# Query halves, transposed probabilities and attention's output of the first sub-blocks: copied by ScalarE instead of VectorE, under new order strings

## The chip, the cores and the metric

One core of one Trainium2 chip runs the program. The time is that of one execution on the device, in microseconds (us). Engines: PE (TensorE: matmuls; PEld are its weight loads), DVE (VectorE), ACT (ScalarE), POOL (GpSimd) and SP, whose queue issues most DMAs.

## What is computed

Chunked attention with 8 memory keys feeds a gated mixing layer and a feed-forward layer with a residual. Batch 4, sequence 768, model width 512, 8 heads of 64.

```python
for c in range(nc):                                   # chunks of 32 queries
    q_c = q[:, :, c_start:c_end]
    k_full = np.concatenate([mem_k, k_ctx], axis=2)   # 8 + 16 + 32 + 8 keys
    v_full = np.concatenate([mem_v, v_ctx], axis=2)
    scores = scale * np.matmul(q_c, k_full.transpose(0, 1, 3, 2))
    scores = scores - np.max(scores, axis=-1, keepdims=True)
    a = np.exp(scores)
    a = a / (np.sum(a, axis=-1, keepdims=True) + 1e-09)
    out[:, :, c_start:c_end] = np.matmul(a, v_full)
...
gate = 1.0 / (1.0 + np.exp(-gate_pre))                # gate_pre: 5 taps over time
x = gate * (x @ w_val) @ w_out
...
xn = (x - mu) / np.sqrt(var + 1e-06) * g_ln
ch = np.maximum(xn @ w_ch1, 0.0) @ w_ch2
return (x + ch).astype(np.float32)
```

## The kernel before

The sequence is cut into 24 sub-blocks of 128 tokens (n = 0 to 23). They form blocks: block 0 is sub-block 0, block 1 is sub-blocks 1 and 2, block 2 is 3 and 4, block 3 is 5 and 6, and so on. Each block goes through attention, mixing (`mix_steps`) and the feed-forward layer (`ch1` fills c_ps, `second` fills acc).

Matmuls of later blocks take float16 halves: each value is a high and a low half, and three products stand for one. The weights arrive as 64-bit numbers in 20 pieces of 1 MB. Each piece is made a 32-bit one (`to_f32`: ScalarE L239, then VectorE L240), goes into a sum of squares (`gram`: matmuls that add into a Gram matrix, whose trace `weight_scale` takes on VectorE as diag, L293, and a column, L294, and sums on PE, L301), and is split into halves (`split_weight`: ScalarE L310, VectorE L311). While that goes on, the first blocks work on 32-bit data: attention of sub-blocks 0 to 4 (`attention32`), mixing of blocks 0 and 1, the feed-forward layer of block 0 (its input is xnf).

`attention32` copies the queries into a block-diagonal tile bd (two halves of 64 partitions: the first by ScalarE at L482, the second by VectorE at L484 unless `n in BD`), takes scores (s_ps) on PE, exponentials (sc), transposes the probabilities on PE (pT_ps, L498), copies them to pT (VectorE L505, or ScalarE if `n in PT`), and multiplies them with the values (pv, L515). `activations` writes pv out to xT in four pieces of 64 partitions: two by ScalarE (L413); the other two by ScalarE if `n < EVAC_ACT or n >= NEVAC`, else by VectorE (L415). `split_values` uses the same function for sub-blocks 5 and later, with a scale.

At the start, and behind the first scores, the program has fills: 120 matmuls on a tile of ones (L269) whose result nobody reads (32 + 64 + 8 + 16, `FILLS`).

What sets the order: the program is recorded in the order of `PLAN`, and then `pin` chains the instructions of each engine in an order that is written out as a string per engine (`ORDER`). A letter in it is the stream that an instruction belongs to (a and b: attention of even and odd sub-blocks, x and y: mixing, f and g: feed-forward, m, p, q: weights, s: set-up), a number how many follow, and `+n` takes one from further back in its stream. Each engine executes its string strictly in order.

Of the kernel before, what the change touches and what calls it, by code (L numbers as in the profile page):

```python
# [54 lines left out]
ORDER = {
    "PE": (
        "s24a+16a+16a+16a+16a+16a+16a+16a+16a+16a+16a+16a69a+4a+4a+4a+4a+4a+4a+4a+4a+20a+20a+20a+20a+20a+20a+20a+20a+20a+20a+20"
        "a+20a+20a+20a+20a+20a20m16m+16x14b16x2m8x4m8a16b14s8p8b6p16a4mx4p16a16f3f+13f+13f+13f13p8y3f6p8y13p8y2pb17y6f20gf15g5q16"
        "b4gaf4a16qg4b16ff+23g3f23a4g2a16bf23g12f27x12b48f21g6f24g6x7f36x29g11f12gx6ax18f12g6b48f12g24a48g30f48a48bg18f72b48y36"
        "g24ay12g6f24b48y24a48g6f36g12f12g6a48g24bx12f48x12f48x24b48f48g30af36b48g12f12a48x24g60bg12a48g54f96g10b48g20y24f48y24a"  # L60
        "f24g12b48f24a48y24g30bg66a48g30b48x24f60x12f12x12f24g18f48g12ag24b48f12g18a48x24f36g30bg42a48g24f24b48f60y12g10f12y36g32"
        "f36ag12f24b48f24a48y24g6f12g42bg36a48g30b48f96x36f12x12f12g10f12g8f12g12ag24b48f36a48x24f12g60bg54a48f72b48f24y48f12g10"
        "f24g20f12b48ag24f24a48y18f12y6f12g18ba48g96f96b48g10x24g8x24f48g12ag24b48f24g6a48x24f24g78ba48g30f96g10b48y48g32f24g18"
        "f24b48g24y24f12g12f36x48g72f96g42f48g18x12f12g42f36g36f36g6f48g12f12g12f60g48f36g48"),
    "DVE": (
        "sa4s3a5m2bm+2m+2mxx+3xx+2xx+1x3x+3xx+2x4mx2mb2pb2abm+2mbmxpxaxbaxpxax2axax5maxp2axmp2a2b+3yy+3yy+2myy+1y2pyy+3yqyy+1yqym"
        "yqy2mp3mp4bq2b+2b2ypbmy2mybyqybymya+3ybypy2qybypyqypybqpq2x+20qyqaa+2a2q2paq2ayaqapaqb2pqax+22gqb3fbqb3a2b2afqtxtxty+20x"
        "bx2bfb+6btxfx+2xx+1tt+2xtfxbxtxtxbtxtxtbtfxbtx2qxa2t+1t3btxtax2txt+2xax2tx3fax3ax2ab2xaxa+8xatafxa3ta2t2atbt2y+22gt+1tgf"
        "b3fb3a2bt2ytby2fy2tytytx+20y2y+3aybtbyy+1y2tt+1bytbtfbyfbta2tyabya2bya2b2taa+7t+1tyfay2x+22at2yay2ay2ayayty3tay3tt+2tyf2"
        "ybt3yaxgtbtb2txtxt+1x2gy+20xbxtb3fxfxfx+3f2bxfx+2xb+7x2b2f3bf2b2xbfxx+1ba2xafafa3fafa+7xfa2ba4fxax5y+22x10f3xf3b2xy2b2"  # L70
        "y+2yy+1bg4g+1g2babf3x+20f2bfb+8b2fy2fyfyb4yf2y2by2fby2a3fayfy+1a3f2ay2fa+8x+22a2fa4yaby3aby3b2fy5fy4f3yb3fb2yag2b+7b2gxg"
        "g+1g2xx+2xx+1b3xfxfxf3bxx+3fx2x+1x3f6bxy+20a3x+1xaxa4f2a+7fa2bfay+22afa2x7fx6ax4b4f5xfb4g4g+1g2yayb+7y+2f2yy+1fyf2byby2"
        "y+3yfyy+1y3f3bfbyfb2fby+1a2ya6f2yfa+7f2a2fa4by5x+20x+22y9ay2f2b2yfb4f2byfbgxg3g+1g2b+8baxx+2f2bf3xx+1fx3b2x2f2xbfxfbx2f"
        "x2bfbxx+1a5f2af2ax2faa+8a2fa5xbx2y+20xax12f3xy+22f2b2fbxb4g4g+1g2y2y+2aybfb+7fbfby+1y2fyfyx+20b2fy+3b2y2y+1f5y2byfyy+1y2"
        "a3f2a5f2a+7fa2ba4fx+22ay8by2by6f2bfbfybfx2x+2yfxx+1bx2g4g+1g2bxbf5afb+7b2fbxbf2bx+3xbfxx+1xfxbxy+20fxx+1a4f2a2fxf2a2a+7a"
        "xa3fa2x11ax2y+22x4bf5b4xbfg4g+1gx+20gy2bf2bay+2byf3b+8b2fy+1y4y+3byfyb4fy+1yfy2byfy+1f2y2x2yf3yf2xx+1y3x2y5by6fyf5yfx+2x"
        "x+1xg4g+1g2f6xfx+1xfx2f3x5f2x14f3xf10g4g+1gf2g5"),
    "Activation": (
        "s3asam3a4x2bx2mpxbaxp3ab3p3bb+1a2y3pqymm+1q2fbyqq+2qmpya+1q+1qbypqmfaq+1qpq+1qfpypqb+3pfyqpaq2b+3b2pqfqb2qa2b2fbxaqfb+2x"
        "abfxt+1a2ftxfqx3t+1bta2xfxt+1b2atfa+2x2ab2at+1btbf2ab2a2ybb+2fy3t+1tf2aba2y2ba3yb2fa+2t+1ty2ab3fat+1yfta4yax2b2t+1btbx2"  # L80
        "f+1f2b+2f3afba2fxbf+1fx2fa3a+2b6afxaxb2f+1f2x3fxa4y2b2gybab+2f+1f6ba2yafbf+1f2ya3y2b4a+2b2fbaybyf+1af2b2y2bfya2ya3gb+2x3"
        "bf+1f2xf4bxa2faf+1fxfxa3a+2b6axbxfbaf+1x2f2bxbxfa4bgyb+2a2y2f+1fyf2bf3a2yfbyf+1ya3f2a+2b4fbabyf+1yb2fafy2b2y2fba5gxb+2x"
        "a3f+1f3xbfxf3bxf+1f2a2x2aa+2b3fb2af+1xbaxfbfbx3fxb3ga4y3af+1yf2b+2a3bf4bfyf+1y2f2b2a3a+2b4fabay2bf+1f2aby2a3x2y2fb2gb+2a"
        "f+1f6ax2b2afaxf+1f2xa3b4a+2xfax2bf+1afx2fb3x2fa3b2ga2y2bb+2f+1f3bf2y2fbyfb2y2b2f+1x2f2by2xfy2f+1fxfy2fgf+1f7x3f+1f2x3f"
        "f+1f5gf2"),
    "Pool": (
        "s2as2s+2s2ab2a+1ab4atga+1ba2b3a+1a2bab2"),
    "SP": (
        "s+1s3w2l2w2l2w2lw4l3wqw2lqwql2wlqay2ay2a+1a2gb+2ab+2b+2b2x2a+2x2a+2a+2a2b+2b+2gb3ga+2a+2a+2a2y4b+2b+2g2b+2b2a+2a+2a+2a2"
        "x4b+2b+2gb+2b2a+2a+2ga+2a2y4b+2b+2gb+2b2ga+2a+2a+2a2x4b+2b+2b+2bg2ba+2a+2a+2a2y4b+2b+2b+2b2g2a+2a+2a+2a2x4b+2b+2b+2b2a+2"  # L90
        "g2a+2a+2a2y4b+2g2b+2b+2b2a2x4b2g2y4g2x2g4"),
}
# [1034 lines left out]
```

## Time and profile before

| | |
|---|---|
| median of 3 runs | 715.03 us (713.51 to 715.72) |
| the profiled execution's own time | 715.32 us |
| its span, first to last instruction | 713.2 us |
| PE busy | 699.4 us, 98% |
| VectorE busy | 617.2 us, 87% |
| ScalarE busy | 466.4 us, 65% |

The busy share is an average over stages. A matmul of 32-bit data stands in the trace as two records. The span's first 100 us hold the loading and the conversion of the weights; what is read from the trace there is in the rows below, of which each group says what its columns are.

### The profile page before, as it was taken

Reading aid. Unit: us, or ns where it says so; the run is one execution under the profiler, and the core shown is the slowest. Engines: PE = TensorE matmul, PEld = TensorE weight load, DVE = VectorE, ACT = ScalarE, POOL = GpSimd, SP = SyncE. Lnnn points to the kernel's source line nnn. Section 1 sums busy time; section 2 is a strip of 40 time slices with the busy share of each in tenths; the row PEclk is TensorE's granted clock in tenths of the full one; section 3 lists DMA queues with packets and bytes.
Section 4 is the critical chain, followed back from the end, with each engine's and each line's share of the span. In section 5 each row is a group of like instructions: output and inputs, shape, how many; then the busy total and the mean of one; then the engine's idle time right before and its main releaser. Section 6 shows DMA issues by size and latency. Waiting matters only on the chain.

```text
span 713.2 us, 18043 instructions
## 1 busy us (share of the span) xinstructions
PE 699.4 (98%) x7581; PEld 566.8 (79%) x7581; DVE 617.2 (87%) x1341; ACT 466.4 (65%) x746; POOL 16.5 (2%) x37
## 2 busy tenths in 40 slices
PE   8799999999999999999999999999999999999998
PEld 7697668657568788888888878878888878878897
DVE  4999999999999989989889998989988978866643
ACT  3679986556666885873875786677784765553330
POOL 2010010000000000000000000000000000000000
PEclk9999999999999999999999999999999999999999
DMA  9998232041423322323322332232233120111001
GB/s 346 417 409 336 60 96 98 16 112 53 113 59 97 82 46 83 81 55 90 91 52 68 86 73 68 74 83 68 65 87 90 31 31 17 46 17 45 1 17 46
DMA packets 64449, 67.76 MB, mean 95 GB/s; under 512 B 47856, under 2 KB 48112, under 8 KB 64368
## 3 DMA queue, kind: packets, MB, share of 16 engines
q1 hardware_dynamic: 64080, 66.59, 31.0%
q8 instruction: 59, 0.97, 0.6%
q14 instruction: 22, 0.18, 0.1%
q10 hardware_dynamic: 288, 0.02, 0.0%
HBM read 49.30 MB, written 6.29 MB: 78 GB/s over the span
## 4 chain that ended last, share of the span: by engine, by line
PE 73%; DVE 17%; ACT 4%; DMA 3%; issue 2%; DVEq 0%; SPq 0%; ACTq 0%
PE c_ps L839 31%; PE acc L804 19%; PE yps L654 7%; PE val L636 7%; PE acc L884 4%; DMA xn<-xh 3%; PE s_ps L367 2%; DVE gt L618 2%; DVE w L240 2%; DVE w L311 2%; PE pv L449 2%; PE idle L269 1%; ACT spare L239 1%; DVE hb L853 1%; ACT w L310 1%
## 5 line engine op out<-in xcount | busy, mean ns | idle before, releaser
L839 PE MATMUL c_ps<-xn,w 128*128 128x256 f16 (+1 forms) x2304 | 254.0, 268 | 1.3 <-DMA xn<-xh 1.2
L839 PEld LDWEIGHTS <-w 128*128 128x128 f16 x2304 | 216.0, 98 | 31.4 <-DMA xn<-xh 2.2
L618 DVE SCALAR_TENSOR_TENSOR gt<-xT,cw_sb,gt 128x256 f32<-128x256 f32 (+1 forms) x208 | 89.0, 459 | 2.4 <-ACT gt L614 1.5
L804 PEld LDWEIGHTS <-hb 128*128 128x128 f16 x756 | 73.0, 98 | 11.5
L804 PEld LDWEIGHTS <-w 128*128 128x128 f16 x756 | 73.1, 98 | 9.4
L804 PE MATMUL acc<-w,hb 128*128 128x256 f16 (+1 forms) x360 | 64.9, 278 | 0.0
L752 ACT ACTIVATE ft<-c_ps 128x512 f32<-128x512 f32 x72 | 40.8, 593 | 36.5 <-DVE y L822 12.0
L884 PE MATMUL acc<-w,hb 128*128 128x512 f16 (+2 forms) x280 | 64.1, 373 | 0.0
L804 PE MATMUL acc<-w 128*128 128x256 f16 x342 | 58.9, 273 | 0.0
L636 PE MATMUL val<-x,wv 128*128 128x256 f16 (+1 forms) x528 | 58.8, 268 | 0.0
L654 PE MATMUL yps<-wo,hg 128*128 128x512 f16 x252 | 56.5, 379 | 0.0
L804 PE MATMUL acc<-spare,hb 128*128 128x256 f16 (+1 forms) x324 | 54.7, 276 | 0.0
L636 PEld LDWEIGHTS <-wv 128*128 128x128 f16 x528 | 49.3, 98 | 6.1 <-issue 0.2
L804 PE MATMUL acc<-spare,w 128*128 128x256 f16 x324 | 53.5, 273 | 0.0
L654 PEld LDWEIGHTS <-hg 128*128 128x128 f16 x252 | 24.0, 98 | 27.3 <-DVE hg L642 0.2
L762 ACT ACTIVATE hb<-ft 128x1024 f16<-128x1024 f32 x18 | 19.0, 1054 | 32.7 <-DVE ft L761 32.6
L884 PEld LDWEIGHTS <-hb 128*128 128x128 f16 x264 | 25.5, 98 | 18.3
L413 ACT ACTIVATE xT<-pv,c_pv 64x256 f32<-64x256 f32 x70 | 29.3, 461 | 8.8 <-PE pv L449 8.4
L762 ACT ACTIVATE w<-ft 128x1024 f16<-128x1024 f32 x18 | 18.9, 1052 | 20.4 <-DVE ft L761 20.2
L569 ACT ACTIVATE bd<-qt,s 64x512 f16<-64x512 f32 x38 | 27.2, 715 | 3.7 <-DVE s L209 3.2
L570 DVE SCALAR_TENSOR_TENSOR bd<-qt,s,bd 64x512 f16<-64x512 f32 x38 | 28.3, 744 | 0.6
L763 DVE TENSOR_TENSOR w<-ft,w 128x1024 f16<-128x1024 f32 x18 | 22.0, 1223 | 6.7 <-ACT w L762 6.7
(192 smaller groups left out, 1200.0 us busy)
## 6 DMA issues: line engine op xcount, KB each, us to landing
vt<-in_v_dram SPq DMA_DIRECT2D x24, 512.0 KB, 4.1
...
```

The costliest lines, as they stand in the source:

```text
L413: nc.scalar.activation(out=o, in_=t[pp, :, :, e, :], func=AF.Copy, scale=c_pv if isinstance(c_pv, float) else c_pv[pp])
L569: nc.scalar.activation(out=hi, in_=src, func=AF.Copy, scale=s[pp, 0:1])
L570: nc.vector.scalar_tensor_tensor(out=lo, in0=src, scalar=s[pp, 0:1], in1=hi, op0=ALU.mult, op1=ALU.subtract)
L618: nc.vector.scalar_tensor_tensor(out=o, in0=xT[:, hp, 0:n, kk:kk + SUB], scalar=cw_sb[:, kk, hp:hp + 1], in1=o, op0=ALU.mult, op1=ALU.add)
L636: nc.tensor.matmul(out=t[:, u, 0:T], lhsT=l, rhs=r, start=(x == 0), stop=(x == len(todo) - 1))
L654: nc.tensor.matmul(out=t, lhsT=l, rhs=r, start=(x == 0), stop=(x == len(todo) - 1))
L752: nc.scalar.activation(out=ft[:, at:at + 2, :].rearrange("p x (m n) -> p m x n", m=2), in_=t.rearrange("p (m x n) -> p m x n", m=2, x=2), ...
L762: nc.scalar.activation(out=o[0][1], in_=ft, func=AF.Copy)
L763: nc.vector.tensor_tensor(out=o[1][1], in0=ft, in1=o[0][1], op=ALU.subtract)
L804: nc.tensor.matmul(out=o, lhsT=l, rhs=r, start=first, stop=(p == half // 2 - 1 and u2 == 1 and end[t] == x))
L839: nc.tensor.matmul(out=t[:, u * T:(u + 1) * T], lhsT=l, rhs=r, start=(x == 0), stop=(x == len(todo) - 1))
L884: nc.tensor.matmul(out=a[:, 0:n], lhsT=l, rhs=r, start=(first and x == 0), stop=(end and x == len(todo) - 1))
```

## The change

Three tables are set so that sub-blocks 0 to 4 copy both query halves (`BD`) and the transposed probabilities (`PT`) on ScalarE, and so that all pieces of attention's output from sub-block 2 on go to ScalarE (`NEVAC` 2; before, sub-blocks 2 to 7 sent two of four to VectorE): 5 + 5 + 12 = 22 instructions. The order strings of PE, VectorE, ScalarE and SP are new for roughly the first quarter of the program; behind that, and on GpSimd, the order is the same. `EXP8` and `OWN` are empty, so the code that they would switch on is not used.

```diff
-NEVAC = 8
+NEVAC = 2
 NXH = 4
-PT = ()
-BD = ()
+PT = (0, 1, 2, 3, 4)
+OWN = {}
+EXP8 = ()
+BD = (0, 1, 2, 3, 4)
...
     "DVE": (
-        "sa4s3a5m2bm+2m+2mxx+3xx+2xx+1x3x+3xx+2x4mx2mb2pb2abm+2mbmxpxaxbaxpxax2axax5maxp2axmp2a2b+3yy+3yy+2myy+1y2pyy+3yqyy+1yqym"
+        "sa3s3a4m2m+2m+2mxx+3xx+2xx+1x3x+3xx+2x3mxpxb2xmm+2b2m3bpxbxpxax2ax6ax2axa2p2m3xmp2yy+3yy+2yy+1y3y+3ypyy+1y2qyq2pyp2ymp4b"
...
     "Activation": (
-        "s3asam3a4x2bx2mpxbaxp3ab3p3bb+1a2y3pqymm+1q2fbyqq+2qmpya+1q+1qbypqmfaq+1qpq+1qfpypqb+3pfyqpaq2b+3b2pqfqb2qa2b2fbxaqfb+2x"
+        "s2a+1sasamam2a4x3b+1xmpbxa2bpxp2bapb3apbpa4y4b+1b+1pqmm+1q2ybqfq+2mqpba+1fq+1qpyqq+1ypqa2q+1qyfpmqpyfbb+5pb+5qab4pqb2qpq"
```

The start of ScalarE's queue. w_113 and spare are buffers with raw pieces of the weights, g_one (L930 before, L942 now) is an exponential of one column, DMAHW3 the semaphore of the queries' DMA. Before:

```order
L930 ACT_TABLE_LOAD
L930 ACTIVATE g_one<-ones 128x1 [waits DVE_49]
L482 ACTIVATE bd<-qt 64x16x32 [waits DMAHW3_49,Pool_49]
L239 ACTIVATE spare<-cw_raw 128x20 [waits DMAHW1_49]
L380 ACTIVATE sc<-sc 128x512 [waits DVE_49]
L239 ACTIVATE spare<-w_113 128x1024 [waits DMAHW4_49,Pool_49]
L239 ACTIVATE spare<-w_113 128x1024 [waits DMAHW6_49,DVE_49,Activation_49]
```

Now:

```order
L494 ACT_TABLE_LOAD [waits DMAHW3_49]
L494 ACTIVATE bd<-qt 64x16x32 [waits Pool_49]
L942 ACTIVATE g_one<-ones 128x1 [waits DVE_49]
L494 ACTIVATE bd<-qt 64x16x32
L242 ACTIVATE spare<-cw_raw 128x20 [waits DMAHW1_49]
L391 ACTIVATE sc<-sc 128x512 [waits DVE_49]
L242 ACTIVATE spare<-w_113 128x1024 [waits DMAHW4_49,Pool_49]
L515 ACTIVATE pT<-pT_ps 128x512 [waits PE_49]
L242 ACTIVATE spare<-w_113 128x1024 [waits DMAHW6_49,DVE_49,Activation_49]
```

A query copy stands ahead of g_one, the load of the activation table stands ahead of that copy with the wait for the queries, the second query half is here too, and pT stands between the first two pieces of the weights.

VectorE's queue from the first probabilities (sc) to the first taps of the gate (gt). Before:

```order
L394 TENSOR_TENSOR sc<-sc,rs 128x512
L505 COPY pT<-pT_ps 128x512
L240 SCALAR_TENSOR_TENSOR wv<-w_113,spare 128x1024 x2
L484 COPY bd<-qt 64x16x32
L293 TENSOR_TENSOR diag<-gram,eye 128x128
L294 TENSOR_REDUCE wv_col<-diag 128x1
L240 SCALAR_TENSOR_TENSOR wo<-w_113,spare 128x1024
L618 SCALAR_TENSOR_TENSOR gt<-xT,cw_sb,gt 128x128 x16
```

Now:

```order
L406 TENSOR_TENSOR sc<-sc,rs 128x512
L243 SCALAR_TENSOR_TENSOR wv<-w_113,spare 128x1024 x2
L296 TENSOR_TENSOR diag<-gram,eye 128x128
L297 TENSOR_REDUCE wv_col<-diag 128x1
L243 SCALAR_TENSOR_TENSOR wo<-w_113,spare 128x1024
L630 SCALAR_TENSOR_TENSOR gt<-xT,cw_sb,gt 128x128 x15
```

The two copies are gone from between, and the conversions follow the probabilities directly.

PE's queue around the trace of the last weight (gram<-w_col) and the fourth sub-block's output (pv). Before:

```order
L498 MATMUL pT_ps<-eye,sc 128x128 x4
L884 MATMUL acc_961<-w_113,hb 128x512
L220 LDWEIGHTS ones
L220 MATMUL tot<-ss,ones 128x1
L839 MATMUL c_ps<-xnf,w_112 128x128 x4
L367 MATMUL s_ps<-kt,bd 64x64 x16
L301 LDWEIGHTS ones
L301 MATMUL gram<-w_col,ones 128x1
L884 MATMUL acc_961<-w_113,hb 128x512 x4
L515 MATMUL pv<-pT,vt 128x64 x16
```

Now:

```order
L510 MATMUL pT_ps<-eye,sc 128x128 x4
L896 MATMUL acc_961<-w_113,hb 128x512
L851 MATMUL c_ps<-xnf,w_112 128x128 x4
L896 MATMUL acc_961<-w_113,hb 128x512 x2
L223 LDWEIGHTS ones
L223 MATMUL tot<-ss,ones 128x1
L896 MATMUL acc_961<-w_113,hb 128x512 x3
L304 LDWEIGHTS ones
L304 MATMUL gram<-w_col,ones 128x1
L370 MATMUL s_ps<-kt,bd 64x64 x16
L527 MATMUL pv<-pT,vt 128x64 x16
```

The scores have moved behind the trace, and four acc matmuls that stood between the trace and pv now stand ahead of the trace.

## Rows read from the trace of the kernel before

**Rows 1.** Stretches: length; busy of PE, PEld, DVE, ACT, POOL; clock, DMA share, GB/s.

```profile
20.00:30.00 10.00, 8.53 (x80) 6.14 (x79) 9.83 (x27) 5.30 (x8) 0.00 (x0) 1.00 1.02 416
...
60.00:70.00 10.00, 10.00 (x74) 6.49 (x73) 9.78 (x20) 10.00 (x14) 0.00 (x0) 1.00 0.76 278
...
80.00:90.00 10.00, 9.31 (x87) 6.26 (x87) 9.79 (x23) 9.16 (x14) 0.00 (x0) 1.00 0.38 80
```

**Rows 2.** Timeline of PE: start, length, what, count [idle before <- releaser].

```profile
1.05 3.91 PE L269 MATMUL idle<-ones 128*128 128x128 bf16 x35 [1.05 <-DVE ones L924]
5.71 1.97 PE L367 MATMUL s_ps<-kt,bd 128*64 128x64 f32 x32 [0.75 <-ACT bd L482]
7.62 6.07 PE L269 MATMUL idle<-ones 128*128 128x128 bf16 x77
13.53 1.11 PE L498 MATMUL pT_ps<-eye,sc 128*128 128x128 f32 x8
15.42 2.00 PE L515 MATMUL pv<-pT,vt 64*128 64x64 f32 x32 [0.78 <-DVE pT L505]
...
19.22 0.16 PE L301 MATMUL gram<-wv_col,ones 128*128 128x1 bf16 x1 [0.78 <-DVE wv_col L294]
...
26.27 3.70 PE L654 MATMUL yps<-wo,gt 128*128 128x512 f32 x8 [1.47 <-DVE gt L638]
...
34.58 1.33 PE L515 MATMUL pv<-pT,vt 64*128 64x64 f32 x20 [1.69 <-DVE pT L505]
...
44.52 4.51 PE L839 MATMUL c_ps<-xnf,w 128*128 128x128 f32 x38
...
85.77 0.16 PE L301 MATMUL gram<-w_col,ones 128*128 128x1 bf16 x1 [0.69 <-DVE w_col L298]
85.80 3.68 PE L884 MATMUL acc<-w,hb 128*128 128x512 f32 x8
...
100.22 2.00 PE L515 MATMUL pv<-pT,vt 64*128 64x64 f32 x32 [0.68 <-issue]
```

**Rows 3.** Groups by form, 0 to 180 us: count, busy us, mean ns, idle before.

```profile
L505 DVE COPY pT<-pT_ps 128x512 f32<-128x512 f32 x5 | 3.4, 687 | 2.6 <-PE pT_ps L498 2.6
L415 DVE TENSOR_SCALAR xT<-pv 64x256 f32<-64x256 f32 x6 | 2.3, 424 | 0.1
L484 DVE COPY bd<-qt 64x512 f32<-64x512 f32 x5 | 2.1, 424 | 4.2 <-DMA qt<-in_q_dram 4.0
L413 ACT ACTIVATE xT<-pv 64x256 f32<-64x256 f32 x14 | 4.6, 367 | 2.1 <-PE pv L515 1.9
L482 ACT ACTIVATE bd<-qt 64x512 f32<-64x512 f32 x5 | 3.1, 621 | 1.9 <-DMA qt<-in_q_dram 1.9
L851 ACT ACTIVATE hb<-c_ps 128x512 f32<-128x512 f32 x4 | 2.3, 571 | 0.0
```

**Rows 4.** Timeline of ScalarE, start of the program.

```profile
1.66 1.28 ACT L930 ACT_TABLE_LOAD   x1 [1.66 <-PEq L1115]
2.95 0.20 ACT L930 ACTIVATE g_one<-ones 128x1 f32<-128x1 bf16 x1
5.03 0.63 ACT L482 ACTIVATE bd<-qt 64x512 f32<-64x512 f32 x1 [1.88 <-DMA qt<-in_q_dram]
```

**Rows 5.** Stretches, L269 (fills) alone: length; PE, PEld, clock, DMA, GB/s.

```profile
7.70:10.00 2.30, 2.30 (x23) 2.30 (x24) 1.00 1.00 404
10.20:11.60 1.40, 1.40 (x29) 1.40 (x27) 1.00 1.06 427
```

**Rows 6.** Timeline of VectorE, columns as in rows 2.

```profile
11.37 0.69 DVE L394 TENSOR_TENSOR sc<-sc,rs 128x512 f32<-128x512 f32 x1
14.67 0.69 DVE L505 COPY pT<-pT_ps 128x512 f32<-128x512 f32 x1 [2.61 <-PE pT_ps L498]
...
18.55 0.29 DVE L293 TENSOR_TENSOR diag<-gram,eye 128x128 f32<-128x128 f32 x1 [0.46 <-PE gram L286]
...
42.45 0.68 DVE L693 TENSOR_TENSOR xnf<-xnT,g_sb 128x512 f32<-128x512 f32 x1
```

More of the change, by code (lines that the diff above doesn't have):

```diff
@@ L56 @@
     "PE": (
[L57 to L60, printed above, removed]
@@ new lines @@
+        "a+20a+20a+20a+20a+20a+20a4m8a16m8m+16s8x6m8x8b16m8x6a16mb4p24b16x4a4p8a16p16f3f+13f+13f+13f3y6p8y3f16p8q8y7fq8bpyb16yf10"
+        "ygy5gf6gf18b4gf4g2ag3qa16b16f12f+12f+12f+12f+12f+12f+12f+12f+12f+12f+12f+12f+12f24g2a4g3a16bf29g2f19x12g5x15b48f36g19x12"
+        "f7x9f17g2f12g9x6agx18f24g24b48g12a48g24f48a48bg12f48b48y36g18y12f60ag6b48y6f12g6y6a48y12f24g30a48bg24x12f60x12f36b48x24"
+        "f48g30af36b48g12f12a48x24g60bg12a48g54f96g10b48g20y24f48y24af24g12b48f24a48y24g30bg66a48g30b48x24f60x12f12x12f24g18f48"
@@ new lines @@
+        "g12ag24b48f12g18a48x24f36g30bg42a48g24f24b48f60y12g10f12y36g32f36ag12f24b48f24a48y24g6f12g42bg36a48g30b48f96x36f12x12f12"
+        "g10f12g8f12g12ag24b48f36a48x24f12g60bg54a48f72b48f24y48f12g10f24g20f12b48ag24f24a48y18f12y6f12g18ba48g96f96b48g10x24g8"
+        "x24f48g12ag24b48f24g6a48x24f24g78ba48g30f96g10b48y48g32f24g18f24b48g24y24f12g12f36x48g72f96g42f48g18x12f12g42f36g36f36g6"
+        "f48g12f12g12f60g48f36g48"),
+    "DVE": (
+        "sa3s3a4m2m+2m+2mxx+3xx+2xx+1x3x+3xx+2x3mxpxb2xmm+2b2m3bpxbxpxax2ax6ax2axa2p2m3xmp2yy+3yy+2yy+1y3y+3ypyy+1y2qyq2pyp2ymp4b"
+        "b+2b3x+20q2pmbmypyqy2byqy5by3by3pyqpq4ypyqmq2aa+2qa3pqapaqa2x+22qpqfbqb3fy+20b2qb3gxaxqxf2x2qxx+2xx+1x2bx2bb+6bt2btxtxt"
+        "t+2tbfxt3xtbtx2tbtxt+1atabfat2xftx2txaxtx2t+2x2axtx2axt2x3faxaa+8xa2xa5t2atbty+22tgt+1tgfb3fb4t2ytybytay2tfy2by2tbx+20"
+        "y+3t2t+1byt2yy+1tyfb2ybtytt+1bfybya4yt2x+22aya3a+7taftyaby2ayayay2ay6ay2tytt+2tyftfyt2yt2atb2txgbxt+1xbx2by+20xb2xtx2x+3"
+        "xx+2xfbf4gx2fb+7b2f3bf2b2xbfxx+1ba2xafafa3fafa+7xfa2ba4fxax5y+22x10f3xf3b2xy2b2y+2yy+1bg4g+1g2babf3x+20f2bfb+8b2fy2fyfy"
+        "b4yf2y2by2fby2a3fayfy+1a3f2ay2fa+8x+22a2fa4yaby3aby3b2fy5fy4f3yb3fb2yag2b+7b2gxgg+1g2xx+2xx+1b3xfxfxf3bxx+3fx2x+1x3f6bx"
+        "y+20a3x+1xaxa4f2a+7fa2bfay+22afa2x7fx6ax4b4f5xfb4g4g+1g2yayb+7y+2f2yy+1fyf2byby2y+3yfyy+1y3f3bfbyfb2fby+1a2ya6f2yfa+7f2"
+        "a2fa4by5x+20x+22y9ay2f2b2yfb4f2byfbgxg3g+1g2b+8baxx+2f2bf3xx+1fx3b2x2f2xbfxfbx2fx2bfbxx+1a5f2af2ax2faa+8a2fa5xbx2y+20xa"
+        "x12f3xy+22f2b2fbxb4g4g+1g2y2y+2aybfb+7fbfby+1y2fyfyx+20b2fy+3b2y2y+1f5y2byfyy+1y2a3f2a5f2a+7fa2ba4fx+22ay8by2by6f2bfbfyb"
+        "fx2x+2yfxx+1bx2g4g+1g2bxbf5afb+7b2fbxbf2bx+3xbfxx+1xfxbxy+20fxx+1a4f2a2fxf2a2a+7axa3fa2x11ax2y+22x4bf5b4xbfg4g+1gx+20gy2"
+        "bf2bay+2byf3b+8b2fy+1y4y+3byfyb4fy+1yfy2byfy+1f2y2x2yf3yf2xx+1y3x2y5by6fyf5yfx+2xx+1xg4g+1g2f6xfx+1xfx2f3x5f2x14f3xf10g4"
+        "g+1gf2g5"),
@@ L216, in upper, with totals @@
         return cols.bitcast(BF16).rearrange("p (n w) -> p n w", w=2)[:, :, 1]
-    def totals(cols, n):
-        t = ps_c.tile([P, 512], F32, tag="c", name="tot") if fast[0] else bank([P, 512], "tot")
+    def totals(cols, n, tag=None):
+        t = ps_a.tile([P, 512], F32, tag=tag, name="tot") if tag else ps_c.tile([P, 512], F32, tag="c", name="tot") if fast[0] else bank([P, 512], "tot")
         nc.tensor.matmul(out=t[:, 0:n], lhsT=ones, rhs=upper(cols), start=True, stop=True)
@@ L371, in scores, with exponentials @@
         return t
-    def exponentials(i, s_ps, c_exp):
+    def exponentials(n, i, s_ps, c_exp):
         sc = at.tile([P, 2 * HP, NSEEN], F32, tag="sc", name="sc")
@@ L378, in exponentials @@
         nc.vector.tensor_reduce(out=mx, in_=s_ps, axis=AX.X, op=ALU.max)
+        if n in EXP8:
+            down = sm_p.tile([P, 2 * HP, 1], F32, tag="rs", name="down")
+            sm = sm_p.tile([P, 2 * HP, 1], F32, tag="sum", name="sum")
+            nc.vector.tensor_scalar(out=down, in0=mx, scalar1=-c_exp, scalar2=None, op0=ALU.mult)
+            for x in range(2 * HP):
+                nc.scalar.activation(out=sc[:, x, :], in_=s_ps[:, x, :], func=AF.Exp, scale=c_exp, bias=down[:, x, :],
+                                     accum_out=sm[:, x, :])
+            return sc, sm
         nc.vector.tensor_tensor(out=sc, in0=s_ps, in1=mx.to_broadcast(WIDE), op=ALU.subtract)
@@ L385, in exponentials, with normalize @@
             nc.vector.memset(by_group[64:128, :, 1, NSEEN - RIGHT:NSEEN], 0.0)
-        return sc, by_group
-    def normalize(sc, by):
-        sm = sm_p.tile([P, 2 * HP, 1], F32, tag="sum", name="sum")
+        return sc, None
+    def normalize(sc, by, sums=None):
+        sm = sm_p.tile([P, 2 * HP, 1], F32, tag="sum", name="sum") if sums is None else sums
         rs = sm_p.tile([P, 2 * HP, 1], F32, tag="rs", name="rs")
-        nc.vector.tensor_reduce(out=sm, in_=sc, axis=AX.X, op=ALU.add)
+        if sums is None:
+            nc.vector.tensor_reduce(out=sm, in_=sc, axis=AX.X, op=ALU.add)
         nc.vector.tensor_scalar(out=sm, in0=sm, scalar1=1e-9, scalar2=by, op0=ALU.add, op1=ALU.mult)
@@ L416, in activations, with split_values @@
                                             op0=ALU.mult)
-    def split_values(n, d, u, i, sc, s, c_pv):
+    def split_values(n, d, u, i, sc, s, c_pv, sums=None):
         vt = sub[n]["v"]
-        normalize(sc, 2.0 ** -PSCALE)
+        normalize(sc, 2.0 ** -PSCALE, sums)
         p2 = [at.tile([P, 2 * HP, NSEEN], F16, tag=f"p{r}", name=f"p{r}") for r in range(2)]
@@ L489, in attention32 @@
         yield
-        sc, by_group = exponentials(i, s_ps, float(D) ** -0.5)
+        sc, sums = exponentials(n, i, s_ps, float(D) ** -0.5)
         yield
         if n >= PV16:
-            yield from split_values(n, d, u, i, sc, s, c_pv)
+            yield from split_values(n, d, u, i, sc, s, c_pv, sums)
             return
-        normalize(sc, 1.0)
+        normalize(sc, 1.0, sums)
         t = bank([P, HP, P], "pT_ps")
@@ L579, in attend @@
         yield
-        sc, by_group = exponentials(i, s_ps, c_exp)
+        sc, sums = exponentials(n, i, s_ps, c_exp)
         yield
-        yield from split_values(n, d, u, i, sc, s[:, 2:3], c_pv)
+        yield from split_values(n, d, u, i, sc, s[:, 2:3], c_pv, sums)
     blk = {}
```

36 lines of the change are left out of this document (11 added, 25 removed).

## The prediction

> **What bounds the kernel now.** Read first the table of stretches [rows 1]: its columns are busy time and count for PE, its weight loads, VectorE, ScalarE and GpSimd, then the granted clock. VectorE is full from 20 us on (9.83 of 10), when PE still has breaks (8.53); at 60 us PE, VectorE and ScalarE are all full, and at 80 nearly so. So no share of busy time tells which of them sets the end. The PE timeline does [rows 2]: its brackets give the idle time ahead of a group. After the first scores at 5.71 us six waits are longer than 0.6 us: 0.78 (for the probabilities' copy pT), 0.78 (the trace of the first weight), 1.47 (gate times value), 1.69 (the next two pT copies), 0.69 (the trace of the last weight) and 0.68 us, together 6.1 us. All stand ahead of 101 us. Behind that PE has work in front of it nearly always, and the order there is the same in both kernels once the new strings have run out. PE's work does not change: the same matmuls, the same 120 fills. The end therefore moves by what PE's waits and the pace of its early matmuls change, and by nothing else. That 11 us leave VectorE is not a gain by itself.
>
> **What is moved.** VectorE loses five copies of query halves at 424 ns, five copies of transposed probabilities at 687 ns and twelve evictions of attention's output, at least 424 ns each [rows 3]: 2.1 + 3.4 + 5.1 = 10.6 us. ScalarE takes the same 22 instructions at 621, 571 (the nearest row of its own from PSUM at that size) and 367 ns [rows 3]: 3.1 + 2.9 + 4.4 = 10.4 us. About 7 us of this falls ahead of 101 us, the rest in stretches where PE never waits; I cost the rest at nothing, since both engines keep slack there in which 0.4 us evictions disappear. GpSimd's order is the same, and SP's queue only exchanges neighbours among its loads.
>
> **Term 1, the first scores come later: +1.9 us (0.9 to 2.9).** Before, the activation table is loaded at 1.66 us, while the first queries are still on their way; the queries land at 5.03 us, ScalarE copies one half (0.63 us) and VectorE the other at the same time, and the scores start at 5.71 [rows 2, 4]. In the new order a query copy is ScalarE's first activation. The table load goes in front of it, and the wait for the queries' DMA stands on the load. So from the landing there follow in one queue the load 1.28, the first half 0.63, the exponential of one column 0.20 and the second half 0.63, where 0.63 stood before [rows 4]: 2.1 us more, 2.0 with a little overlap of neighbours. The scores then start at about 7.7.
>
> Behind them stand fills, and the transposition pT_ps follows only when these have run, at 13.53, although the probabilities were ready on VectorE at 12.06 [rows 2, 6]. The fills run at two paces [rows 5]: 23 in 2.30 us (0.10 us each) up to 10.0 us, 29 in 1.40 us (0.05 each) from 10.2. At 128 columns that is the 1.2 and the 2.4 GHz level, though the column of the granted clock has 1.00 for both. If the rise moves with the scores, everything shifts by 2.0, less the one fill (0.1) that now stands ahead of the scores: 1.9. If it comes at 10.1 us as before, some 20 fills that ran at 0.10 run at 0.05, and the shift is 0.9. If it comes 2 us later still, another 20 run slow: 2.9. I take the middle, because PE's work ahead of the fills has the same form and is only later.
>
> The Trainium skill (ScalarE: Activation LUTs, "What ACT_TABLE_LOAD costs") gives a load 1283 ns and a drain of about 1380 ns more, 2.66 us in all. The trace agrees on the load and shows no drain: the next activation begins 0.01 us behind it [rows 4]. By the page's sum this term would be about 1.4 us larger and the time 717.2.
>
> **Term 2, the way from the first pT to the first feed-forward matmul: -1.3 us (-1.0 to -1.8).** Before, pT is copied by VectorE and the two conversions of the first weight queue behind it, so that the trace's first step (diag) comes at 18.55, 5.0 us after pT_ps began [rows 2, 6]. Now the first conversion runs on VectorE while PE still fills, and eight Gram matmuls cover ScalarE's copy, where PE waited 0.78 us. But the second conversion can't start sooner: its ScalarE half stands behind the pT copy in ScalarE's queue, and that copy waits for PE. I credit 0 to 0.3 us. From diag to the end of the normalized input xnf (18.55 to 43.13) VectorE ran almost without a pause [rows 1, 6]. Of that queue a query half (0.42) and two pT copies (0.69 each) go away, 1.8 us, and three one-column operations are moved into it; one output product is put behind a weight conversion, so that a short wait appears. I take 1.3 for the whole. What follows xnf is even: c_ps began 1.4 us after it [rows 2], and now one more conversion and its Gram matmuls stand between, which is work that PE did later before.
>
> **Term 3, 44 to 102 us: +0.2 us (-1.4 to +1.8).** Here PE lost 0.69 and 0.68 us [rows 2], 1.4 in all, which is the most to be gained. In the new PE order the fourth sub-block's output matmuls (pv) stand right behind the trace of the last weight and the scores; the four matmuls of 3.68 us that stood between [rows 2] are gone as cover. Their pT is now copied in ScalarE's queue, which is full in that stretch (10.00 of 10 us at 60, 9.16 at 80) [rows 1] and carries two more query copies of 0.62 and this one of 0.57 ahead of pv [rows 3], 1.8 us. That is the upper bound. The wait for the last trace should shrink, since VectorE has 1.8 us less ahead of it; the next pT has three matmuls as cover. So one wait is exchanged for another, with a small loss.
>
> **Sum.** +1.9 - 1.3 + 0.2 = +0.8 us. The profiled execution took 715.32 us, 2.1 more than its span of 713.2 and 0.3 above the median of 715.03; these add to each kernel alike. I set the sum on the median: 715.8 us. With each term at its bounds it is 712.7 to 718.7.
>
> **Rivals.**
> *The relief reaches PE* (faster). VectorE is what five of the six waits name or stand behind, and it was full in the whole stretch. If the new order is as dense as the old one and 7 us are gone from it, all six waits close, and 6.1 - 1.9 = 4.2 us are gained: 710.8, or about 712 if a third stays. For it: each wait follows a VectorE row. Against it: the pT copies sit in a queue of ScalarE that waits for PE and is itself full later. Chance 0.20.
> *The clock rises later and the whole start slips* (slower). Before, the rise came 9 us after the first fill, with a wait of 0.75 us between; now PE has nothing for some 2.8 us ahead of the scores. If the 9 us count from the scores, nearly all 76 fills run at 0.10, from 9.6 to about 17.2: the shift is 3.7 instead of 1.9, the time 717.6. It decides for slower from a shift of 3.3 on. The Trainium skill (TensorE: Matmul & The Clock Gate, "Part 1: The HAM clock gate") says that the gate follows how busy the engine has lately been; by it a longer pause makes a late rise likelier, and the trace shows one rise only. A late pT on ScalarE at its bound (+1.8) leads to the same side. Chance 0.23.
> *The change doesn't hold the start* (no change). If the load is done while the queries are on their way, as before, only the second half in the same queue counts, 0.6: the time is about 714.5. Against it: the wait stands on the load. Chance 0.07.
>
> **How the numbers follow.** The forecast has 0.50. A measurement of this kernel can tell about 0.3%, 2.1 us, from no change (712.9 to 717.2); the forecast and the third rival lie within it, 0.57. Faster by more is the first rival, 0.20, slower by more the second, 0.23. The range reaches down to 711.8, which leaves out half of the first rival, and up to 718.8, which holds the bounds of the terms and leaves out 0.08.
>
> **What would show it.** In the profile after: the table load at about 5.0 us and the first scores near 7.7 (term 1; scores near 6.3 would refute it); pT_ps between 14.5 and 16.5 (beyond 17: the second rival); no wait of PE at the first pv, and c_ps from xnf about 0.6 us later than 44.5 (before 43: the first rival); a wait ahead of the fourth pv that names ScalarE. The prediction is wrong if PE's waits past 100 us change, or if VectorE stays full in spite of the copies it lost.

## The result and the profile after

The kernel after takes 718.25 us (median of 6 runs, 717.17 to 720.69) against 713.78 us before: a ratio of 1.0064 [1.0041, 1.0086]. In twelve later runs it is 718.66 against 715.0, 1.0046 [1.0030, 1.0062]. So the change costs 3 to 5 us. The forecast was 715.8, no change: the side is wrong, the range (711.8 to 718.8) holds the time. It was added to 715.03, the median of the three runs known then; the six runs have 713.78.

Timeline of ScalarE in the kernel after, columns as in [rows 4], which it answers:

```profile
5.18 1.28 ACT L494 ACT_TABLE_LOAD   x1 [5.18 <-DMA qt<-in_q_dram]
6.48 0.63 ACT L494 ACTIVATE bd<-qt 64x512 f32<-64x512 f32 x1
7.12 0.20 ACT L942 ACTIVATE g_one<-ones 128x1 f32<-128x1 bf16 x1
7.23 0.61 ACT L494 ACTIVATE bd<-qt 64x512 f32<-64x512 f32 x1
...
17.52 0.60 ACT L515 ACTIVATE pT<-pT_ps 128x512 f32<-128x512 f32 x1 [4.24 <-PE pT_ps L510]
```

The load waits for the queries' DMA and everything stands behind it, in the order that the prediction named. Timeline of PE (compare [rows 2]):

```profile
7.94 1.98 PE L370 MATMUL s_ps<-kt,bd 128*64 128x64 f32 x32 [2.86 <-issue]
9.85 6.69 PE L272 MATMUL idle<-ones 128*128 128x128 bf16 x76
16.38 1.11 PE L510 MATMUL pT_ps<-eye,sc 128*128 128x128 f32 x8
...
18.17 2.00 PE L527 MATMUL pv<-pT,vt 64*128 64x64 f32 x32 [0.23 <-ACT pT L515]
...
46.90 2.23 PE L851 MATMUL c_ps<-xnf,w 128*128 128x128 f32 x18
...
80.05 1.14 PE L510 MATMUL pT_ps<-eye,sc 128*128 128x128 f32 x8
...
87.19 0.17 PE L304 MATMUL gram<-w_col,ones 128*128 128x1 bf16 x1
89.17 1.15 PE L370 MATMUL s_ps<-kt,bd 128*64 128x64 f32 x32 [1.82 <-ACT pT L515]
...
157.42 0.28 PE L851 MATMUL c_ps<-xn,w 128*128 128x256 f16 x1 [0.55 <-DMA xn<-xh]
```

The transposition pT_ps comes at 16.38 instead of 13.53, the first feed-forward matmul at 46.90 instead of 44.52, the trace of the last weight at 87.19 instead of 85.77. Right behind that trace PE waits 1.82 us: the fifth sub-block's scores want the PSUM bank of the fourth pT, and ScalarE has not copied it yet. ScalarE's timeline shows what stands ahead:

```profile
86.50 1.13 ACT L313 ACTIVATE w<-w,gs_sb 128x1024 f16<-128x1024 f32 x1
87.53 0.61 ACT L710 ACTIVATE xh<-xh 128x512 f16<-128x512 f32 x1
88.06 0.57 ACT L863 ACTIVATE hb<-c_ps 128x512 f32<-128x512 f32 x1
88.53 0.58 ACT L515 ACTIVATE pT<-pT_ps 128x512 f32<-128x512 f32 x1
```

PE had finished that pT_ps at about 81.2. The stretches of [rows 1] now read (same columns):

```profile
20.00:30.00 10.00, 7.41 (x101) 6.63 (x99) 9.13 (x23) 8.00 (x16) 0.00 (x0) 1.00 1.02 412
60.00:70.00 10.00, 10.00 (x82) 6.88 (x81) 9.01 (x21) 9.98 (x15) 0.11 (x1) 1.00 0.50 174
80.00:90.00 10.00, 8.18 (x60) 4.96 (x61) 8.57 (x16) 10.00 (x16) 0.00 (x0) 1.00 0.23 40
```

VectorE is no longer full (9.83, 9.78 and 9.79 before); ScalarE is, at 60 and 80 us. The moved copies cost what was put down for them [rows 3]: groups by form, 0 to 180 us:

```profile
L425 ACT ACTIVATE xT<-pv 64x256 f32<-64x256 f32 x20 | 6.7, 372 | 0.3 <-PE pv L527 0.2
L494 ACT ACTIVATE bd<-qt 64x512 f32<-64x512 f32 x10 | 6.2, 619 | 0.1
L515 ACT ACTIVATE pT<-pT_ps 128x512 f32<-128x512 f32 x5 | 3.0, 593 | 6.2 <-PE pT_ps L510 6.0
```

The fills' two paces (compare [rows 5]; columns: length, PE, PEld, clock, DMA, GB/s):

```profile
10.00:13.70 3.70, 3.70 (x37) 3.70 (x36) 1.00 1.03 406
13.80:16.30 2.50, 2.39 (x40) 2.15 (x39) 1.00 1.02 399
```

They run at 0.10 us until about 13.7 us, 3.6 us longer than before (10.1).

### The profile page after: what moved, and what is told of

Its sections match the earlier page's. It is cut to its first block, busy times and chain, and to the rows that moved or that the text cites. A ratio compares the mean times of both kernels' runs of the same rounds, so it can differ in the third digit from the quotient of the medians.

```text
span 716.1 us, 18046 instructions
## 1 busy us (share of the span) xinstructions
PE 699.8 (98%) x7581; PEld 567.1 (79%) x7581; DVE 609.5 (85%) x1319; ACT 476.2 (67%) x768; POOL 14.8 (2%) x37
## 4 chain that ended last, share of the span: by engine, by line
PE 69%; DVE 11%; ACT 7%; DMA 3%; issue 1%; DVEq 0%; ACTq 0%
PE c_ps L851 29%; PE acc L816 19%; PE yps L666 7%; PE val L648 6%; PE acc L896 4%; DMA xn<-xh 2%; PE s_ps L370 2%; PE pv L461 2%; ACT w L313 2%; DVE gt L630 1%; DVE w L314 1%; ACT spare L282 1%; ACT xT L425 1%; ACT spare L242 1%; DMA pT<-p 1%
## 5 line engine op out<-in xcount | busy, mean ns | idle before, releaser
L425 ACT ACTIVATE xT<-pv,c_pv 64x256 f32<-64x256 f32 x76 | 32.0, 462 | 5.8 <-PE pv L461 5.4
```

Source lines behind the costliest of these rows:

```text
L425: nc.scalar.activation(out=o, in_=t[pp, :, :, e, :], func=AF.Copy, scale=c_pv if isinstance(c_pv, float) else c_pv[pp])
```

## Experiments

Three reasons were on the table. A: the late start, behind the load of the activation table and ScalarE's second query half. B: the fourth pT in ScalarE's full queue. C: TensorE's clock, which a pause of PE makes rise later or fall again, so that a pause costs more than its length. All ratios are to the kernel before, run on the same chip; in the table one per mille is 0.7 us.

| kernel | ratio [95%] | first scores, pT_ps, last trace (us) |
|---|---|---|
| before (profile above) | 1 | 5.71, 13.53, 85.77 |
| before once more | one execution | 5.63, 11.46, 85.65 |
| after | 1.0064 [1.0041, 1.0086] | 7.94, 16.38, 87.19 |
| after once more | 1.0046 [1.0030, 1.0062] | 7.86, 15.14, 85.93 |
| load early | 1.0031 [1.0015, 1.0048] | 6.58, 12.35, 83.31 |
| and second half on VectorE | 1.0011 [0.9999, 1.0022] | 5.68, 11.46, 83.07 |
| before with load late | 1.0046 [1.0029, 1.0063] | 7.01, 14.08, 87.92 |
| fourth pT on VectorE | 1.0053 [1.0039, 1.0068] | 7.63, 16.01, 86.84 |
| start and fourth pT undone | 1.0000 [0.9990, 1.0010] | 5.66, 11.77, 83.76 |
| fills ahead of the scores | 1.0043 [1.0026, 1.0060] | 7.69, 13.46, 84.26 |
| load early, fills at 83 us | 1.0016 [1.0004, 1.0028] | 6.45, 12.22, 83.13 |
| fills at both places | 1.0048 [1.0032, 1.0064] | 7.78, 13.55, 84.37 |
| start repaired | 1.0004 [0.9990, 1.0018] | 5.73, 11.51, 82.95 |
| start, pT, xn repaired | 1.0021 [1.0005, 1.0038] | 5.62, 11.39, 85.18 |

**The kernel after with the table load early.** ScalarE's queue:

```diff
 ACT_TABLE_LOAD
-ACTIVATE bd<-qt 64x16x32
 ACTIVATE g_one<-ones 128x1
-ACTIVATE bd<-qt 64x16x32
+ACTIVATE bd<-qt 64x16x32 x2
```

> The changed kernel with one move in ScalarE's order: the exponential of one column stands ahead of the query copies again, so that the table load does not wait for the queries. Both halves are still copied by ScalarE. Theory A (the start sets the loss: what delays the first pT_ps delays the end nearly one for one): table load at 1.7 us, scores at about 6.4 instead of 7.94, pT_ps at 14.6 to 15.2 instead of 16.38, time 1.0 to 1.7 us below the changed kernel. Theory B (the loss comes from ScalarE's fuller queue between 44 and 102 us, where a late start is absorbed): less than 0.4 us below it.

By the ratios it is 1.1 to 2.4 us better than the kernel after, and still slower than before. In this execution the clock had risen before the scores, so that pT_ps came at 12.35, earlier than expected. Its PE timeline and, below it, its stretches (columns as in [rows 1]) show what ate the rest in the profiled execution:

```profile
85.28 1.15 PE L366 MATMUL s_ps<-kt,bd 128*64 128x64 f32 x32 [1.80 <-ACT pT L511]
86.36 3.43 PE L523 MATMUL pv<-pT,vt 64*128 64x64 f32 x32
89.73 7.24 PE L847 MATMUL c_ps<-xn,w 128*128 128x256 f16 x48
```

```profile
80.00:85.00 5.00, 3.48 (x10) 1.26 (x8) 4.41 (x9) 5.00 (x8) 0.00 (x0) 1.00 0.27 52
85.00:90.00 5.00, 4.72 (x66) 4.47 (x67) 5.00 (x14) 4.44 (x9) 0.00 (x0) 0.67 0.59 107
90.00:95.00 5.00, 5.00 (x32) 3.83 (x31) 4.16 (x6) 4.96 (x10) 1.93 (x2) 0.65 0.50 184
```

Behind the wait the granted clock falls from 1.00 to its half level (1.2 GHz) for part of both stretches, and the same pv takes 3.43 us instead of 2.00, the same 48 c_ps 7.24 instead of 5.41: 3.3 us on top of a wait of 1.8. Seven of this kernel's twelve executions have a mean granted clock of 0.995 or less.

**The second query half back on VectorE as well.** One copy goes back (`BD = (1, 2, 3, 4)`), with the load early.

> The changed kernel with the start of before: sub-block 0's second query half is copied by VectorE again, and the table load does not wait for the queries. Theory A: scores at 5.7 to 5.9 us, pT_ps at 13.5 to 14.3, time 2.0 to 2.9 us below the changed kernel. Theory B: less than 0.5 us below it; the wait of 1.82 us at 89 us stays in either theory.

1.0011: most of the loss is gone, so A is the larger part (the gap to the load early alone is 0.0020, and the intervals overlap a little). The rows show what stays, a new wait at 24 us for a query half behind a weight conversion, and B's wait (no fall of the clock in this execution):

```profile
24.00 1.15 PE L366 MATMUL s_ps<-kt,bd 128*64 128x64 f32 x32 [2.03 <-ACT bd L490]
...
85.02 1.15 PE L366 MATMUL s_ps<-kt,bd 128*64 128x64 f32 x32 [1.79 <-ACT pT L511]
```

**The kernel before with the load late.** The reverse, alone:

```diff
 ACT_TABLE_LOAD
-ACTIVATE g_one<-ones 128x1
 ACTIVATE bd<-qt 64x16x32
+ACTIVATE g_one<-ones 128x1
```

> The kernel before with one move: ScalarE's copy of the first query half stands ahead of the exponential of one column, so that the table load waits for the queries; VectorE still copies the other half. Theory A: scores at about 7.1 us instead of 5.71, pT_ps 1.3 us or more later than 13.53, time 1.0 to 2.0 us above the kernel before. Theory B: within 0.4 us of it.

1.0046, about 3.3 us, against 1.0 to 2.0 expected: exchanging two activations costs as much as the whole change in its second measurement. In the profiled execution pT_ps moved by only 0.55 us against the first profile of the kernel before (14.08), c_ps by 2.7 (47.19). Between them it is the clock again: behind the usual 1.69 us wait for pT at 35.14, the stretches read

```profile
35.00:40.00 5.00, 4.86 (x57) 4.48 (x58) 4.83 (x19) 1.59 (x5) 0.00 (x0) 0.71 1.00 402
40.00:45.00 5.00, 5.00 (x40) 4.92 (x39) 3.78 (x5) 4.84 (x6) 0.28 (x2) 0.60 1.02 414
```

where the first profile of the kernel before, behind the same wait [rows 2], has 1.00 in both stretches. Three of this kernel's six executions have a mean clock below 0.997 (0.990 to 0.995); of the 79 executions of the kernel before that ran beside the experiments, two do. But the two fastest executions (716.3 us, mean clocks 0.999 and 0.997) are still 2.2 us above the kernel before (714.06), so the clock's later falls are not the whole cost.

**The fourth pT back on VectorE.** The kernel after with one copy back (`PT = (0, 1, 2, 4)`), ahead of the low half of a normalized input (xh).

> The changed kernel with the fourth sub-block's pT copied by VectorE again, put where VectorE waits 0.76 us at 82 us. The start is that of the changed kernel. Theory A: the wait of 1.82 us ahead of the scores at 89 us shrinks to 0.3 or less, time 0.7 to 1.3 us below the changed kernel, since part comes back at the next transposed input. Theory B: the whole 1.8 us or more is gained, since ScalarE's queue is the cause of the loss.

The wait at the scores is gone, and no gain can be told (1.0053 lies between the two ratios of the kernel after): PE arrives earlier at the next input, the transposed xn, which is not there yet.

```profile
91.09 0.27 PE L847 MATMUL c_ps<-xn,w 128*128 128x256 f16 x1 [1.07 <-DMA xn<-xh]
91.77 6.97 PE L847 MATMUL c_ps<-xn,w 128*128 128x256 f16 x47 [0.41 <-DMA xn<-xh]
```

B alone is not the cause: one wait of 1.8 us becomes two of 1.5 together, with a slow c_ps behind them (6.97 us for 47; granted clock 0.68 from 90 to 95 us).

**Fills ahead of the scores.** The kernel after with 26 more fills in PE's pause, to test C against A.

```diff
-FILLS = (32, 64, 8, 16)
+FILLS = (58, 64, 8, 16)
```

> The kernel after, with 26 more fills (matmuls on ones that nobody reads) ahead of the first scores; the table load stays behind the queries, so the scores still start at about 7.9 us. If what costs is the granted clock (PE has nothing for 2.86 us ahead of the scores and its clock rises to full only at 13.75 us), the clock rises earlier, some 30 fills run at 0.05 instead of 0.10 us, pT_ps starts at 14.2 to 14.8 instead of 16.38, and the median is 715.8 to 716.8 instead of 718.25. If it is the table load alone, that is the scores' own delay of 2.2 us, nothing is gained: pT_ps at 16 to 16.4, median 718.0 to 718.6. If the filled start draws the clock down later, it is above 719.

The mechanism is there: all fills behind the scores run at the fast pace and pT_ps is back at 13.46 although the load is late, and the trace of the last weight comes 2.9 us earlier.

```profile
7.69 1.15 PE L366 MATMUL s_ps<-kt,bd 128*64 128x64 f32 x32 [0.75 <-issue]
8.78 4.85 PE L268 MATMUL idle<-ones 128*128 128x128 bf16 x76
13.46 1.11 PE L506 MATMUL pT_ps<-eye,sc 128*128 128x128 f32 x8
...
84.26 0.17 PE L300 MATMUL gram<-w_col,ones 128*128 128x1 bf16 x1
```

The median does not follow (1.0043, just under the two ratios of the kernel after). In the profiled execution the clock fell behind the wait at 86 us, as above (0.77 and 0.54 in the stretches of 5 us from 85; pv 3.31 us, c_ps 7.36), and the gain was spent there.

**Load early, and fills in the wait at 83 us.** 32 matmuls on ones behind the trace of the last weight.

```diff
 nc.tensor.matmul(out=W.acc[:, P:P + 1], lhsT=ones, rhs=upper(col), start=True, stop=True)
+for _ in range(32 if W is W2 else 0):
+    nc.tensor.matmul(out=W.acc[:, 2 * P:3 * P], lhsT=ones, rhs=ones, start=True, stop=True)
```

> The first experiment's kernel (the kernel after with the early table load, 717.27) with 32 fills between the trace of the last weight and the scores behind it, where PE waited 1.80 us for the fourth pT on ScalarE and its granted clock then fell to half for 6.8 us. The wait itself can't shrink. If the clock is what the wait costs, the fall at 87 us goes (48 c_ps in 5.4 us instead of 7.24, pv 2.0 instead of 3.43), most of the 3.3 us that it took comes back in the runs that had it, and the median is 714.3 to 715.3, with the runs closer together. If the wait costs only its own length, the median stays at 716.8 to 717.6. If the fills run past the wait, up to 0.5 us more.

```profile
83.16 1.95 PE L302 MATMUL gram<-ones 128*128 128x128 bf16 x32
85.08 1.15 PE L368 MATMUL s_ps<-kt,bd 128*64 128x64 f32 x32
86.16 2.00 PE L525 MATMUL pv<-pT,vt 64*128 64x64 f32 x32
88.09 5.41 PE L849 MATMUL c_ps<-xn,w 128*128 128x256 f16 x48
```

The wait is as long as before, only filled, and pv and c_ps keep their fast times. None of nine executions has a mean clock below 0.997 (seven of twelve were at 0.995 or less without the fills). That is C shown at this place; the two kernels ran on different chips, but on the chip with the fills the start in another order (below), whose wait is not filled, has three of twelve at 0.995 or less. It is worth about 1 us of the median (1.0016 against 1.0031, intervals that overlap), less than the 2 to 3 us expected.

**Start and fourth pT both undone.** The edits of the second and the fourth experiment together.

> The kernel after with both suspects undone: the first sub-block's second query half is back on VectorE (table load early, scores at 5.7 us) and the fourth pT too. If start and fourth pT add up as measured one by one (-2.9 and -0.3 against 718.25): 714.8 to 715.3, still above the kernel before. If the wait of 1.8 us at 85 us matters only through the clock, which the early start spares in half of the executions: 714.0 to 714.6. If the new wait ahead of the normalized input (1.1 us at 91 us with the fourth pT alone) grows, as VectorE is asked for more: 715.5 to 716.5.

1.0000 [0.9990, 1.0010]; the median of 714.50 us lies in the second of the three ranges. With A and B both gone the loss is gone. How much of that is B's is not shown, since A undone alone has 1.0011 [0.9999, 1.0022]. PE still waits for the transposed xn here (0.99 and 0.46 us at 88 us). What is left of the change (four query halves, four pT copies, twelve evictions off VectorE) neither gains nor loses.

**The start in another order.** The second experiment's kernel, with

```diff
 ACTIVATE sc<-sc 128x512
-ACTIVATE spare<-w_113 128x1024
-ACTIVATE pT<-pT_ps 128x512
 ACTIVATE spare<-w_113 128x1024 x2
+ACTIVATE pT<-pT_ps 128x512
+ACTIVATE spare<-w_113 128x1024
...
-ACTIVATE spare<-spare 128x1024
 ACTIVATE bd<-qt 64x16x32
+ACTIVATE spare<-spare 128x1024
```

on ScalarE, and on PE the second eight Gram matmuls of the first weight ahead of pv.

> The second experiment's kernel (715.34) with the start put into another order: ScalarE's half of the second weight conversion ahead of its first pT copy, all 16 Gram matmuls of the first weight ahead of pv, and the second half of the next queries ahead of the conversion that waits for its DMA. If PE's waits of 0.50, 0.77 and 2.03 us between 15 and 24 us in that kernel are lost time, 1 to 2.5 us come back: 712.8 to 714.3, level with the kernel before or below it. If the stretch is set by the weights' arrival, the same time is waited for later: 715.0 to 715.7.

1.0004: no gain that can be told from the kernel it was made from, none over the kernel before. Nine of its twelve executions lie between 713.5 and 714.6 us, three at 717 with a mean clock of 0.993 to 0.995.

**All repairs.** That kernel, the fourth pT back on VectorE, and the second xh ahead of the last steps of the trace's column.

> The kernel with the repaired start, and the fourth pT back on VectorE, and the second normalized input made before the column of the last trace is finished, so that its transposition starts about 1.3 us earlier. If the three places found so far (start, fourth pT, normalized input) are the whole loss and VectorE's relief is worth anything, PE has no wait over 0.5 us between 80 and 95 us, its clock does not fall there, and the median is 1 to 2.5 us below the kernel before (ratio 0.9965 to 0.9985). If what PE gains there is waited for behind 150 us, the ratio is 0.999 to 1.001.

It missed, 1.0021, and six of its twelve executions have a mean clock of 0.995 or less. In the profiled one the second piece of the first weight landed later: ScalarE's half of its conversion began at 13.23 us instead of 11.53. PE now waits for it with all 16 Gram matmuls ahead of pv and nothing to do, and the clock falls (granted clock 0.75 at 15 to 20 us, 0.57 at 20 to 25):

```profile
12.35 0.63 PE L286 MATMUL gram<-wv 128*128 128x128 bf16 x8
15.89 0.63 PE L286 MATMUL gram<-wv 128*128 128x128 bf16 x8 [2.91 <-DVE wv L240]
16.45 2.78 PE L524 MATMUL pv<-pT,vt 64*128 64x64 f32 x32
```

**Fills at both places.** The kernel after, with nothing but PE kept busy.

> The kernel after with both sets of fills, 26 ahead of the first scores and 32 behind the trace of the last weight; nothing else is changed, the table load is late and the fourth pT is on ScalarE. If the clock is a large part of the loss, the two gains add up: 1.0025 to 1.004 of the kernel before (2 to 3 us), with no execution below a mean clock of 0.996. If the clock is a side issue, it stays at the 1.0043 of the fills at the start, or above.

1.0048, no better than the kernel after on the same chip (1.0046), although no execution has a mean clock below 0.995, where four of the twelve of the kernel after have 0.993 or less. So C is not a cause by itself: pv keeps its 2.00 us, PE runs into the next input, and in this execution the clock falls there instead (0.66 from 90 to 95 us). PE's timeline:

```profile
91.12 6.87 PE L849 MATMUL c_ps<-xn,w 128*128 128x256 f16 x47 [1.49 <-DMA xn<-xh]
...
408.54 0.85 PE L459 MATMUL pv<-pT,vs 64*128 64x64 f16 x46 [1.36 <-DMA pT<-p]
```

**Both kernels once more.**

> The kernel after once more, unchanged, with the other three on one chip. Its ratio to the kernel before should lie between 1.004 and 1.0085 again, so that 3 to 6 us have to be explained. If the granted clock's moves and the waits for transposed inputs behind 150 us are chance of one execution, this profile has them at other places or of other sizes (rise between 5 and 14 us; waits for xn and pT between 1 and 4 us in all); if they belong to the kernel, the rise comes at 13 to 14 us again and the waits stand at 157 us as before.

> The kernel before once more, for a second profile. If the clock's first rise is chance of one execution, it comes at another time than 10.1 us (5 to 14); if it goes with the start of the work, within 1 us of it. Waits of PE of 0.78, 0.78, 1.47, 1.69, 0.69 and 0.68 us up to 101 us again, within 0.1 each; those behind 150 us of other sizes.

The kernel after has pT_ps at 15.14 this time, with a granted clock of 0.78 at 5 to 10 us and 0.87 at 10 to 15: the clock had risen, and fell again behind the pause of 3 us. When it is back varies with the execution (11.2 us here, 13.7 in the first profile), but late it is in all four profiles with a late load and no more fills: some of the fills behind the scores run slow until 9.8 to 13.7 us. Of the eight profiles with scores by 6.6 us, seven have these fills fast throughout; the exception is the first profile of the kernel before. Behind the 1.82 us wait at 87.9 us the clock fell here (0.50 from 90 to 95 us, c_ps 7.66 us), which it did not in the first profile. The waits for xn at 158 us are 0.19 us each.

The kernel before is the telling one. First its second profile, then the one row of the first profile that answers to the third:

```profile
11.46 1.11 PE L498 MATMUL pT_ps<-eye,sc 128*128 128x128 f32 x8
...
43.11 4.51 PE L839 MATMUL c_ps<-xnf,w 128*128 128x128 f32 x38
...
58.87 1.98 PE L654 MATMUL yps<-wo,gt 128*128 128x512 f32 x4 [1.52 <-DVE gt L638]
...
85.65 0.16 PE L301 MATMUL gram<-w_col,ones 128*128 128x1 bf16 x1 [0.56 <-DVE w_col L298]
```

```profile
58.83 1.98 PE L654 MATMUL yps<-wo,gt 128*128 128x512 f32 x4
```

Here the clock rose early, pT_ps came 2.07 us sooner and c_ps 1.41, and at 58.8 us all of it was given back, in a wait for VectorE's product gt. The span is 713.2 us both times. Of the six waits that were expected again within 0.1 us, three came (0.79, 0.77 and 0.68); 1.47, 1.69 and 0.69 became 0.93, 0.78 and 0.56, and one of 0.23 us, at 30 us, became 1.41. In the kernel after there is no such wait at 58 us: from pT_ps to the last trace it takes 70.81, 70.79, 70.83, 70.80 and 70.82 us in five profiles of kernels with its order (after, after once more, fourth pT, fills ahead, fills at both places) whose pT_ps lies between 13.46 and 16.38, where the kernel before takes 72.24 and 74.19. In the last two of the five the clock was at 0.71 and 0.73 from 20 to 25 us, at no cost: waits of 0.39, 0.47 and 0.60 us that PE has behind it in the kernel after (26.8 to 30.2 us) are gone in both.

## Why the prediction was right and wrong

The forecast named a loss of 0.8 us and called it no change. What failed is the size: the start (term 1) slipped by 2.85 us in the profile pair, not by 1.9, the early gain (term 2) was 1.0, not 1.3, and the part behind 101 us, put at nothing, lost 0.8 or 0.9.

What the profile pair lost can be laid against the terms. Give each matmul the usual (median) spacing of its form and take PE's elapsed time less that sum: the difference of the two kernels is how late PE is, net of the order. It is +2.85 us at pT_ps, +1.9 at c_ps, about +2 at 110 us (1.8 to 2.1, as the orders differ around it) and +2.9 at the end (the spans differ by 2.9). The medians of the first measurement differ by more, 4.5 us, because the profiled execution of the kernel before (715.32 us) lies 1.5 above its median; what makes up this rest the pair does not show. That the range holds the time is in part luck: around the six-run median of 713.78 the same sum and width would have ended at 717.6.

**Term 1**, +1.9 (0.9 to 2.9): +2.85, its upper bound in this execution, +1.6 in the second profile of the kernel after. The mechanism is as told: the load at 5.18 (about 5.0 forecast), the scores at 7.94 (7.7). The drain that the Trainium skill (ScalarE: Activation LUTs, "What ACT_TABLE_LOAD costs") adds to a load is not there in this trace either: the query copy begins 0.02 us behind the load. What failed is the clock: the middle was chosen because its rise was taken to move with the scores, which came 2.2 us later; the rise came 3.6 us later, at 13.7 us instead of 10.1, and in other executions at other times. One trace could not show that the rise at 10.1 was itself a late one, or that it does the kernel before no harm: its order gives an earlier start back at 58.8 us, while the new order carries whatever pT_ps has to the last trace.

**Term 2**, -1.3 (-1.0 to -1.8): about -1.0, the smaller bound. The second conversion did stand behind the pT copy, as VectorE's timeline in the kernel after shows (compare [rows 6]), and the first pv waits only 0.23 us.

```profile
19.40 1.23 DVE L243 SCALAR_TENSOR_TENSOR wv<-w,spare 128x1024 int32<-128x1024 int32 x1 [3.96 <-ACT spare L242]
21.43 0.29 DVE L296 TENSOR_TENSOR diag<-gram,eye 128x128 f32<-128x128 f32 x1 [0.80 <-PE gram L289]
...
44.34 0.68 DVE L705 TENSOR_TENSOR xnf<-xnT,g_sb 128x512 f32<-128x512 f32 x1
```

Diag comes 5.05 us after pT_ps, as before (5.02). From diag to the end of xnf it takes 23.6 us (21.43 to 45.02), where it took 24.6 [rows 6]. c_ps is 2.4 us later, 1.9 without the eight Gram matmuls that now stand ahead; 0.6 was forecast.

**Term 3**, +0.2 (-1.4 to +1.8): between 0 and +0.3, right in size. The wait is of the pT copy in ScalarE's queue, 1.82 us, the upper bound given; but it stands one step ahead of where it was put, at the scores that take pT's bank, not at pv. The waits of 0.69 and 0.68 us [rows 2] went, as hoped.

**What was put at nothing**: the part behind 101 us, +0.8 or +0.9, by waits for transposed inputs (0.55 and 0.19 us at 157 us, where the kernel before has none), and the clock's falls behind the 1.8 us wait. A change of PE's waits past 100 us was one of the prediction's own signs of being wrong. Its reading that PE has no wait over 0.6 us there was not right for the kernel before either: that one waits 0.68 us for xn at 324 us. Six of eighteen executions of the kernel after have a mean clock of 0.993 or less, with a median of 720.2 us; the other twelve have 718.0. That lifts the median by about 0.5.

**The rivals.** The third (the start is held) is out by the scores at 7.94. The second (the clock rises later and the start slips, or a late pT at its bound) is the side that came: both happened. The start slipped by 2.85 of the 3.7 us, and the wait for pT reached its bound, which what was gained ahead of it made good. The first (the relief reaches PE) was half right: from pT_ps to the last trace the new order is 1.4 to 3.4 us shorter. With the early start this brings the last trace to 83 us, where the pT and xn waits at 85 to 92 us follow.

**Open.** By the same reckoning the length behind 110 us is 0.7 us below to 1.4 above that of the first profile of the kernel before in nine further profiles, and 2.4 to 3.2 above it in four (load early, and the three with more fills), with waits for transposed xn and pT such as the 1.36 us above. Whether that is chance or belongs to these kernels the runs do not tell, since each has one profile. It may be why gains of 3 us at the trace do not show in the medians.
